# A new order table for all five engines of an attention and MLP kernel

## The chip, the core and the metric

The kernel runs on one core of a Trainium2 chip. The metric is the device time of one execution in microseconds (us). Before the change the median of three runs is 939.87 us (938.67 to 942.12).

TensorE (PE in the profile) multiplies matrices, VectorE (DVE), ScalarE (ACT) and GpSimd (POOL) work on tiles in SBUF and PSUM, and SyncE (SP) issues the DMAs. Each engine runs its own instructions strictly in order, and waits where an instruction's inputs or its buffer aren't ready.

## The reference

The reference has two parts. The first is attention with a window of 32 among 512 local tokens, joined by 32 global tokens that every local token sees and that see all 544. There are 8 batches, 8 heads and a head dimension of 64:

```python
s_ll = scale * np.matmul(q_l, k_l.transpose(0, 1, 3, 2))
s_ll = np.where(np.abs(pos[:, None] - pos[None, :]) <= 32, s_ll, -1000000000.0)
s_lg = scale * np.matmul(q_l, k_g.transpose(0, 1, 3, 2))
out_l = np.matmul(sm(np.concatenate([s_lg, s_ll], axis=-1)), np.concatenate([v_g, v_l], axis=2))
out_g = np.matmul(sm(scale * np.matmul(q_g, k_all.transpose(0, 1, 3, 2))), v_all)
```

Its output, 8 x 544 = 4352 tokens of 512 numbers, goes through an MLP with a cosine gate:

```python
h = x @ w_in          # 512 -> 2048
g = h * np.cos(h)
return g @ w_out      # 2048 -> 512
```

The weights come as 64-bit floats and are decoded on the chip into pairs of 16-bit floats (a high and a low part), and the inputs of most matmuls are such pairs too: a product takes three matmuls (high by high, high by low, low by high).

## The kernel before

**Attention.** A batch is handled as four pairs of heads (p = 0 to 3). Batches 0 and 1 run in the head of the program (functions f_*, fg_* and h_*; batch 0 wholly in 32-bit floats), while the weights are loaded and decoded. Batches 2 to 7 run in a steady pattern beside the MLP. For one pair: SyncE loads q and k (load_qk, L733); VectorE takes their largest magnitude (qk_a, qm at L818); TensorE spreads it over the partitions (spread_b at L796, into a PSUM tile pm_qk); ScalarE makes the high part qa (L857) and VectorE the low part kl (L858); four DMAs put the halves in place (qk_e, L869 to L874). Then, for each of four tiles of queries, TensorE makes the scores ps (sc_a, L1125 and L1126), VectorE adds the mask and takes the minimum mn of the negated scores (sc_b, L1142), which clears the PSUM tile; ScalarE takes the exponential and its sum (sc_c, by table_act at L715); POOL and ScalarE scale and split the result into plx (sc_d, L1171 to L1178); SyncE transposes it by DMA into ptb (sc_e, L1183); and TensorE multiplies by v into acc (av_a, L1215). ScalarE and VectorE write the MLP's input xh and xl (av_b, L1234 and L1235). The values v of a batch come in one load of 1280 KB (load_v, L781), and VectorE takes their maximum in four instructions (v_q, L897).

**MLP.** The tokens are cut into 17 chunks of 256, and the 2048 hidden units into 8 pieces (j). For chunk c and piece j, TensorE runs 24 matmuls into ph (m1_a, L1369); ScalarE and VectorE reduce the argument u of the cosine (m1_b, L1386 and L1387); ScalarE takes a sine (m1_c, L715); VectorE multiplies into gf (L1404), ScalarE rounds it to gh (L1408) and POOL makes the rest gl (L1409). Then 12 matmuls add to the output po (m2_a, L1423 to L1425), and after the last piece VectorE and ScalarE write o (m2_b, L1436 and L1438).

**Buffers.** PSUM has three tiles for ph, two for po and three that attention shares (ps, acc, pm_qk, gps and gacc). A tile is free when the engine that reads it last is done: ph when gf is made, ps when L1142 is done.

**Tables.** Exp and Sin lie in different tables of ScalarE. Wherever the two alternate in its order, the compiler puts in a load of the other table (ACT_TABLE_LOAD, at L715).

**What sets the order.** The body first issues the instructions step by step (a step is one call of one of the functions above). The table ORDER (L21), a line of numbers for each engine, then chains each engine's instructions:

```python
for name, line in ORDER.items():
    mine = [[i for i in step if i.engine == getattr(E_, name)] for step in steps]
    at_, prev, used = defaultdict(int), None, set()
    for word in line.split():
        word, _, times = word.partition("x")
        k, _, i = word.partition(".")
        at_[k] = int(i or at_[k])
        for _ in range(int(times or 1)):
            ins = mine[int(k)][at_[k]]
            at_[k] += 1
            if prev is not None:
                tc.add_manual_dep(ins, prev.name, order, reason="order")
            prev = ins
```

A word such as 23.4x2 means: of step 23, this engine's instruction 4 and the one behind it. So the table sets the place of every instruction, matmul, DMA issue and so on, on its own engine. What an instruction has to wait for on other engines follows from its data and its buffers, as before.

Of the kernel before, what the change touches and what calls it, by code (L numbers as in the profile page):

```python
# [22 lines left out]
        18x4 22x4 23.4 23.0 23.5 23.1x2 23.6 23.3 23.7 27x4 29.4x4 29.0x2 33 33.2 33.1 33.3 29x2 28x8  # L23
        34x8 35 35.4 35.1x3 35.5x2 40.4 49 35 40.0x2 40.5 40.2 40.6x2 40.3 57 39x8 69x4 41x8 74 74.2
        74.1 74.3 108 108.2 64x24 67x24 72x24 91x24 108.1 108.3 106x24 125x24 109 109.4 109.1 109.5
        109.2 109.6 109.3 109.7 135x7 110x2 110.4 110.2x2 110.5x3 135 143x6 112x8 113x4 124 127x4 141x8
        113x4 143x2 135x16 149x3 149.4 149.3 149.5x3 143x16 150 150.4 150.1 150.5 150.2 150.6 150.3
        150.7 151x8 155 155.4 155.1x3 152x8 156x20 157x8 164x8 189x5 189.6x5 189.5 189.11 164x16 170x5
        176x24 208 208.6x2 208.1x2 208.8x2 208.3x2 171x20 195x4 187x24 208 208.10x2 196 196.2 196.1
        196.3 206x19 227x24 229.6 206x5 229 229.0x3 229.8 229.3x2 229.9x3 229.5 250.6x2 250.0x2 250.8x3  # L30
        250.2x4 250.11 204 209x4 274x4 274.6x3 274.4 274.9x2 274.5 274.11 210x2 210.3 210.2 288.6x3
        288.0x6 288.9x3 300x4 300.6x4 300.4 300.10x2 300.5 230 231x8 233 233.2 233.1 233.3 248x24 272x24
        234 234.2 234.1 234.3 303.6 303.0x3 303.7x3 303.3x3 303.10x2 230x35 311x12 251 252x4 313x4 313.6
        313.4 313.7x5 313.5 253x4 251x35 318x5 318.6x2 318.5 318.8x4 325x3 325.6x6 325.3x3 275x12 276x8
        286x24 275x24 349x5 329x2 329.6 329.2x4 329.7x5 289x2 290 349x2 289x2 294x60 333.6x2 333.0x4
        333.8x2 333.4x2 333.10x2 289x32 307x60 319 322 339 339.6 339.1x2 339.7x2 339.3 339.9 349x17
        369x11 379x4 369x4 326x4 330x4 379x17 335x4 340x4 339x2 339.4x2 379x3 369x9 355x4 356x8 357
        351x2 351.6 351.2x2 351.7x3 351.4x2 351.10x2 371x4 372x8 392x24 407x24 421x24 382x4 394x12 433x2
        433.6x2 433.2 433.8x2 433.3x3 433.10x2 395x4 450.6x5 450.0x6 450.11 409x3 410 409 465.6x2
        465.0x4 465.8x4 465.4x2 394x24 431x24 424x3 435x4 424 448x24 463x24 436 451x3 452x4 479 481  # L40
        481.6 481.1x2 481.7x3 481.3x2 481.10x2 481.5 496 496.6x4 496.1x3 496.10 496.4x2 479x14 467x4
        468x8 479x9 482x4 494x19 496.11 494x5 483x8 489x60 451x33 497x2 498 512x24 529x24 497x2 514.6x2
        514.0 514.8x3 514.1x5 514.11 499x4 500 515x12 516x4 531 531.6 531.1x2 531.7 531.3 531.8x2 531.4
        531.10x2 531.5 517x4 544x21 546x4 546.6x4 546.4x2 546.10x2 533x4 562x24 550x4 583x24 544x3 564x3
        564.6 564.3x2 564.7 564.5 564.8x4 515x24 565x2 585.6x3 585.0 585.9x3 585.1x5 565x2 566x8 567 598
        598.6 598.1 598.7x4 598.2x4 598.11 612 612.6x3 612.1x3 612.9x3 612.4x2 596 586x36 587x4 588x8
        596x23 600x4 610x24 630 630.6 630.1 630.7 630.2x3 630.8x3 628x14 613x36 614x4 618x60 628x10
        643x24 631x4 651x24 630 630.5 645.6x4 645.0 645.10 645.1 645.11 645.2x4 632 653.6x3 653.0x3
        653.9x2 653.3x3 653.11 668x2 668.6 668.2 668.7 668.3x3 668.8x4 666x24 646x4 655x4 687x24 703x24
        673x36 674x4 689x3 689.6x2 689.3x3 689.8x3 690x4 689 691x8 705.6 705.0x4 705.7x2 705.4x2 705.9x3  # L50
        716x24 692 730x24 706x4 718.6x3 718.0 718.9x2 718.1 718.11 718.2x4 747x24 707x8 711x60 764x11
        720x4 733x36 734x4 750 732.6x5 732.0x3 732.11 732.3x3 764x13 749.6x3 749.0x2 749.9 749.2 749.10
        749.3 749.11 749.4x2 751 752 766 766.6x3 766.1x2 766.9 766.3x3 751x3 766.10x2 767x4 776x4 772x12
        787x17 774x3 772x12 807x24 787x7 774.6x6 774.3x3 793x36 794x4 789x3 789.6x2 789.3x3 789.8x2
        823x23 810x4 823 811x8 812 789x2 826x4 827x8 831x60 836x24 850x20 809x2 809.6x2 809.2 809.8x3
        809.3x3 809.11 840x4 866x24 850x4 825x5 825.6x4 825.5 825.10x2 838.6 838.0x2 838.7x5 838.2x4 852
        852.6x2 853x6 854x4 881x24 889x10 904x5 852.1x5 852.8x4 853x30 868x12 869x4 870 883x12 884x4
        889x14 891x12 893x4 904x19 906x12 911x36 912x4 925x24 927x12 928x4 929x8 930 941x24 943x12 944x4
# [1669 lines left out]
```

## Time and profile before

| | us |
|---|---|
| median of 3 runs | 939.87 (938.67 to 942.12) |
| the profiled execution | 944.08 |
| its span | 942.3 |
| PE busy | 886.3 (94%) |
| ACT busy | 677.5 (72%) |
| DVE busy | 585.8 (62%) |
| POOL busy | 495.3 (53%) |

The busy times are shares of the span and say nothing yet of which engine is waited for. The program has parts: up to about 50 us the weights are loaded and decoded beside batch 0's attention, up to about 216 us batches 0 and 1 and the first chunks run, then the steady pattern, and from about 792 us on little but the MLP's last chunks. The program has about 7900 matmuls, and each engine's instruction has a line in kernel.py by which the views name it.

### The profile page before, as it was taken

Reading aid. Unit: us, or ns where it says so; the run is one execution under the profiler, and the core shown is the slowest. Engines: PE = TensorE matmul, PEld = TensorE weight load, DVE = VectorE, ACT = ScalarE, POOL = GpSimd, SP = SyncE. Lnnn points to the kernel's source line nnn. Section 1 sums busy time; section 2 is a strip of 40 time slices with the busy share of each in tenths; the row PEclk is TensorE's granted clock in tenths of the full one; section 3 lists DMA queues with packets and bytes.
Section 4 is the critical chain, followed back from the end, with each engine's and each line's share of the span. In section 5 each row is a group of like instructions: output and inputs, shape, how many; then the busy total and the mean of one; then the engine's idle time right before and its main releaser. Section 6 shows DMA issues by size and latency. Waiting matters only on the chain.

```text
span 942.3 us, 20875 instructions
## 1 busy us (share of the span) xinstructions
PE 886.3 (94%) x7892; PEld 611.9 (65%) x7892; DVE 585.8 (62%) x1536; ACT 677.5 (72%) x1331; POOL 495.3 (53%) x731
## 2 busy tenths in 40 slices
PE   5689988789999999999999999989999999999998
PEld 4468745466766776756767667657767766666673
DVE  5998885778765776776676667665765444223230
ACT  4789988779998878967876777767787774444441
POOL 3477889815766455466562546555656552121220
PEclk9779999999999999999999999999999999999999
DMA  9774615875667466476456655645554421000000
GB/s 339 274 235 169 213 23 125 156 192 105 149 146 137 128 120 132 108 158 121 104 127 141 135 99 124 163 85 134 92 109 85 93 42 42 1 23 13 12 24 23
DMA packets 162422, 110.79 MB, mean 118 GB/s; under 512 B 140176, under 2 KB 142608, under 8 KB 160400
## 3 DMA queue, kind: packets, MB, share of 16 engines
q1 hardware_dynamic: 162176, 109.31, 47.8%
q8 instruction: 62, 1.02, 0.4%
q14 instruction: 40, 0.33, 0.1%
q10 hardware_dynamic: 144, 0.13, 0.1%
HBM read 51.61 MB, written 8.91 MB: 64 GB/s over the span
## 4 chain that ended last, share of the span: by engine, by line
PE 48%; ACT 16%; DVE 12%; DMA 10%; POOL 5%; issue 4%; SPq 1%; DVEq 0%; POOLq 0%; ACTq 0%
PE ph L1369 21%; PE po L1425 7%; PE po L1423 7%; PE po L1424 7%; ACT t L715 3%; DMA qkr<-qk 3%; ACT u L715 2%; DMA vr<-v 2%; ACT L715 2%; DVE u L1387 2%; PE acc L1215 2%; DMA ptb<-plx 1%; DVE gf L1404 1%; ACT u L1386 1%; ACT gh L1408 1%
## 5 line engine op out<-in xcount | busy, mean ns | idle before, releaser
L1369 PE MATMUL ph<-xh,wi_h 128*128 128x256 f16 x1024 | 281.5, 275 | 8.5 <-DVE gf L1404 7.5
L1369 PE MATMUL ph<-xl,wi_h 128*128 128x256 f16 x1024 | 281.7, 275 | 0.0
L1369 PE MATMUL ph<-xh,wi_l 128*128 128x256 f16 x1024 | 281.4, 275 | 0.4 <-POOL wi_l L457 0.4
L1409 POOL TENSOR_TENSOR gl<-gf,gh 128x512 f16<-128x512 f32 x136 | 159.4, 1177 | 226.2 <-ACT gh L1408 222.0
L1369 PEld LDWEIGHTS <-wi_h 128*128 128x128 f16 x2176 | 212.0, 99 | 49.5 <-issue 12.1
L1424 PE MATMUL po<-wo_l,gh 128*128 128x512 f16 x544 | 203.9, 379 | 1.5 <-POOL wo_l L457 1.5
L1423 PE MATMUL po<-wo_h,gh 128*128 128x512 f16 x544 | 201.5, 379 | 3.2 <-DVE o L1436 2.3
L1425 PE MATMUL po<-wo_h,gl 128*128 128x512 f16 x544 | 201.5, 379 | 1.6 <-POOL gl L1409 1.6
L1387 DVE SCALAR_TENSOR_TENSOR u<-ph,ca,u 128x512 f32<-128x512 f32 x136 | 101.2, 745 | 114.9 <-ACT u L1386 114.6
L715 ACT ACTIVATE t<-t,mn 128x224 f32<-128x224 f32 (+1 forms) x256 | 118.2, 463 | 51.6 <-DVE mn L1142 35.9
L1171 POOL TENSOR_SCALAR t<-t,sm 128x224 f32<-128x224 f32 (+1 forms) x192 | 85.3, 462 | 127.4 <-DVE sm L1162 104.0
L715 ACT ACTIVATE u<-u,halfpi 128x512 f32<-128x512 f32 x136 | 97.1, 720 | 61.8 <-DVE u L1387 61.2
L1404 DVE SCALAR_TENSOR_TENSOR gf<-u,ph 128x512 f32<-128x512 f32 x136 | 92.8, 684 | 76.5 <-ACT u L715 65.6
L1386 ACT ACTIVATE u<-ph,quarter,ca 128x512 int32<-128x512 f32 x136 | 103.9, 767 | 46.4 <-PE ph L1369 46.1
L1178 POOL TENSOR_TENSOR plx<-t,plx 128x192 f16<-128x192 f32 (+1 forms) x192 | 120.9, 654 | 24.5 <-ACT plx L1176 24.0
L1369 PEld LDWEIGHTS <-wi_l 128*128 128x128 f16 x1088 | 107.4, 99 | 14.5 <-POOL wi_l L457 0.6
L1408 ACT CAST gh<-gf 128x512 f16<-128x512 f32 x136 | 82.6, 614 | 46.2 <-DVE gf L1404 46.1
L1425 PEld LDWEIGHTS <-gl 128*128 128x128 f16 x544 | 53.2, 98 | 67.1 <-POOL gl L1409 2.5
L1424 PEld LDWEIGHTS <-gh 128*128 128x128 f16 x544 | 53.2, 98 | 55.2 <-issue 4.2
L715 ACT ACT_TABLE_LOAD x67 | 86.0, 1283 | 2.6 <-DVE gmn L768 1.4
L1423 PEld LDWEIGHTS <-gh 128*128 128x128 f16 x544 | 52.9, 98 | 52.3 <-issue 2.3
L1142 DVE CUSTOM_DVE_ANT_0 t<-ps,msk,al 128x192 f32<-128x192 f32 (+1 forms) x192 | 76.5, 427 | 9.5 <-PE ps L1126 9.3
(239 smaller groups left out, 1223.5 us busy)
## 6 DMA issues: line engine op xcount, KB each, us to landing
qkr<-qk SPq DMA_DIRECT2D x24, 608.0 KB, 4.5
vr<-v SPq DMA_DIRECT2D x8, 1280.0 KB, 6.6
out<-o SPq DMA_DIRECT2D x33, 256.0 KB, 2.0
kh<-qa SPq DMA_DIRECT2D x48, 152.0 KB, 2.7
wo_h<-wo SPq DMA_DIRECT2D x8, 512.0 KB, 4.5
wo_l<-wo SPq DMA_DIRECT2D x8, 512.0 KB, 4.3
qa<-kl SPq DMA_DIRECT2D x24, 152.0 KB, 2.5
kl<-kl SPq DMA_DIRECT2D x24, 152.0 KB, 3.1
```

The costliest lines, as they stand in the source:

```text
L715: ins = nc.scalar.activation(*a, **k).ins
L1171: nc.gpsimd.tensor_scalar(t[:, h], t[:, h], r[:, h : h + 1], 1.0, op0=ALU.mult, op1=ALU.mult)
L1178: nc.gpsimd.tensor_tensor(lo[:, h], t[:, h], hi[:, h], op=ALU.subtract)
L1369: nc.tensor.matmul(ph[:, a], w[:, kc, f], x[:, kc, q], start=first and ip == 0, stop=last and ip == 2, skip_group_check=True,)
L1386: nc.scalar.activation(u.bitcast(I32), ph, AF.Identity, bias=quarter, scale=a)
L1387: nc.vector.scalar_tensor_tensor(u, ph, a, u.bitcast(I32), op0=ALU.mult, op1=ALU.subtract)
L1404: nc.vector.scalar_tensor_tensor(gf, w, 0.5, st.pop(("ph", c, j)).rearrange("p a b -> p (a b)"), op0=ALU.mult, op1=ALU.mult,)
L1408: nc.scalar.copy(gh, gf)
L1409: ins = nc.gpsimd.tensor_tensor(gl, gf, gh, op=ALU.subtract).ins
L1423: nc.tensor.matmul(po[k], gh[:, q], wo_h[:, f], start=(f == 0), stop=False)
L1424: nc.tensor.matmul(po[k], gh[:, q], wo_l[:, f], start=False, stop=False)
L1425: nc.tensor.matmul(po[k], gl[:, q], wo_h[:, f], start=False, stop=(f == NJ - 1))
```

## The change

Only the numbers in ORDER change, for all five engines. The arithmetic, the tiles, the buffers, the DMAs and the steps are the same. The table is 34 lines longer, so that each line number behind it is larger by 34 in the changed kernel (L1142 is L1176 there). From the middle of the program on, the old table for TensorE is a regular pattern (24 matmuls of one piece, 12 of another, and so on), and the new one is mixed more finely. Two pieces of the table, whose other lines are of the same kind:

```diff
--- before.py
+++ after.py
@@ -20,217 +20,251 @@
 ORDER = {
     "PE": """
-        18x4 22x4 23.4 23.0 23.5 23.1x2 23.6 23.3 23.7 27x4 29.4x4 29.0x2 33 33.2 33.1 33.3 29x2 28x8
-        34x8 35 35.4 35.1x3 35.5x2 40.4 49 35 40.0x2 40.5 40.2 40.6x2 40.3 57 39x8 69x4 41x8 74 74.2
...
+        18x4 22x4 23.4 23.0 23.5 23.1x2 23.6 23.3 23.7 27x4 29x8 33.1 33.3 33.0 33.2 28x8 35 35.4 34x8
+        35.1x3 35.5 40 40.4 40.1 40.5 40.2 40.6x2 49 35 40.3 57 35 39x8 69x4 41x8 74 74.2 74.1 74.3 108
...
     "SP": """
-        0.1 0.0 6 2x2 4x2 1 5 3 7 6 8 9 10 11 12 13.1 13.0 78 14x2 17 79 15.1 15.0 81 77 16.1 172 16.0
-        17 80 172 82 83 84 98 99 100 101 102 103 104 105 122 123 119 175 120 175 121 116 173 174 173 117
...
+        0.1 0.0 1 2x2 3 5 4 8 4 7 6x2 9 10 11 12 13.1 13.0 15 14 77 14 16x2 15 78 81 80 79 172.1 117
+        17.1 84 17.0 82 116 83 98 119 118 100 172.0 99 101 102 104 103 105 120 121 173 175x2 173 122 123
...
```

What that does is shown at three places. The first is SyncE's queue at the start of the program: qkr, qf and kf are the queries and keys of batch 0, msk the mask, and wi and wo the weights, loaded into tiles that are used for other things later. Before:

```order
L777 DMA qkr_0_0_118<-qkf 128x352 x2
L777 DMA qf_0_3_132<-qkf 128x352
L777 DMA qf_0_1_122<-qkf 128x352
L777 DMA kf_0_1_123<-qkf 128x352
L777 DMA qf_0_2_127<-qkf 128x352
L777 DMA kf_0_2_128<-qkf 128x352
L1514 DMA msk_73<-mask 128x896
L583 DMA plx_76<-wi 128x1024
L583 DMA wo_h_92<-wi 128x1024 x2
L777 DMA kf_0_3_133<-qkf 128x352
L583 DMA vhl_77<-wi 128x1024
```

And now:

```order
L811 DMA qkr_0_0_118<-qkf 128x352 x2
L1548 DMA msk_73<-mask 128x896
L811 DMA qf_0_1_122<-qkf 128x352
L811 DMA kf_0_1_123<-qkf 128x352
L617 DMA wo_h_92<-wi 128x1024
L617 DMA plx_76<-wi 128x1024
L811 DMA qf_0_2_127<-qkf 128x352
L617 DMA vhl_77<-wi 128x1024
L811 DMA kf_0_2_128<-qkf 128x352
L617 DMA wo_h_92<-wi 128x1024
```

The mask is issued third instead of eighth, and the first loads of w_in stand among those of q and k.

The second is VectorE round the maximum over batch 7's v (vm4_7 from vr_7), beside the clearing of the scores of batch 6's second pair (ps_6_1_2 and ps_6_1_3) and chunk 10 of the MLP (u_10, gf_10). Before:

```order
L1142 ISA t_6_1_2_8687,mn_6_1_2_8688<-ps_6_1_2_8678,msk_73,al_6_1_8109 128x224
L1142 ISA mn_6_1_2_8688 128x1
L787 TENSOR_SCALAR qm_7_0_9128<-qm_7_0_9128 128x1
L427 TENSOR_SCALAR qm_7_0_9128<-qm_7_0_9128 128x1
L897 TENSOR_REDUCE vm4_7_9543<-vr_7_9079 128x1 x4
L1387 SCALAR_TENSOR_TENSOR u_10_1_8726<-ph_10_1_8701,ca_10_8627,u_10_1_8726 128x512
L901 TENSOR_REDUCE vm_7_9542<-vm4_7_9543 128x1
L787 TENSOR_SCALAR vm_7_9542<-vm_7_9542 128x1
L1142 ISA t_6_1_2_8687,mn_6_1_3_8783<-ps_6_1_3_8778,msk_73,al_6_1_8109 128x192
L1142 ISA mn_6_1_3_8783 128x1
L1142 ISA t_6_1_2_8687,mn_6_1_3_8783<-ps_6_1_3_8778,msk_73,al_6_1_8109 128x192
```

And now the place where the maximum stands:

```order
L1421 SCALAR_TENSOR_TENSOR u_10_4_8993<-ph_10_4_8968,ca_10_8627,u_10_4_8993 128x512
L1176 ISA t_6_2_2_9021,mn_6_2_2_9022<-ps_6_2_2_9010,msk_73,al_6_2_8458 128x224
L1176 ISA mn_6_2_2_9022 128x1
L1470 TENSOR_SCALAR o_9_1_9077<-po_9_1_8424,co_8_8319 128x512
L931 TENSOR_REDUCE vm4_7_9543<-vr_7_9079 128x1 x2
L1421 SCALAR_TENSOR_TENSOR u_10_5_9060<-ph_10_5_9035,ca_10_8627,u_10_5_9060 128x512
L1176 ISA t_6_2_2_9021,mn_6_2_2_9022<-ps_6_2_2_9010,msk_73,al_6_2_8458 128x224
L1176 ISA mn_6_2_2_9022 128x1
L1438 SCALAR_TENSOR_TENSOR gf_10_4_9031<-u_10_4_8993,ph_10_4_8968 128x512
L1389 TENSOR_SCALAR co_12_11271<-osc_99,pvs_101 128x1
L1176 ISA t_6_2_2_9021,mn_6_2_3_9123<-ps_6_2_3_9118,msk_73,al_6_2_8458 128x192
```

The four instructions of the maximum stand behind the scores of the third pair's tile 1 (ps_6_2_1) now, where before they stood ahead of the second pair's tile 3 (ps_6_1_3); they are in two pairs, of which the second comes later still. On SyncE the load of vr_7 stood ahead of kl_6_2's last move and stands behind it now.

The third is ScalarE in chunk 10, with the exponentials of batch 6's second pair (t_6_1) and the sines of chunk 10 (u_10). Before:

```order
L1386 ACTIVATE u_10_0_8661<-ph_10_0_8636,quarter_83,ca_10_8627 128x512
L715 ACTIVATE u_10_0_8661<-u_10_0_8661,halfpi_85 128x512
L715 ACT_TABLE_LOAD
L715 ACTIVATE t_6_1_0_8460,sm_6_1_8794<-t_6_1_0_8460,mn_6_1_0_8461 128x192 x2
L715 ACTIVATE t_6_1_1_8558,sm_6_1_8794<-t_6_1_1_8558,mn_6_1_1_8559 128x224 x2
L1408 CAST gh_10_0_8695<-gf_10_0_8697 128x512
L715 ACTIVATE t_6_1_2_8687,sm_6_1_8794<-t_6_1_2_8687,mn_6_1_2_8688 128x224 x2
L1386 ACTIVATE u_10_1_8726<-ph_10_1_8701,quarter_83,ca_10_8627 128x512
L1234 ACTIVATE xh_6_8786<-acc_6_0_8741,xs_95 128x512
L715 ACTIVATE t_6_1_2_8687,sm_6_1_8794<-t_6_1_2_8687,mn_6_1_3_8783 128x192 x2
L715 ACTIVATE gt_6_0_8464,gsm_6_0_8803<-gt_6_0_8464,gmn_6_0_8465 128x544
```

And now:

```order
L749 ACT_TABLE_LOAD
L749 ACTIVATE u_10_0_8661<-u_10_0_8661,halfpi_85 128x512
L749 ACT_TABLE_LOAD
L749 ACTIVATE t_6_1_1_8558,sm_6_1_8794<-t_6_1_1_8558,mn_6_1_1_8559 128x224 x2
L749 ACTIVATE t_6_1_2_8687,sm_6_1_8794<-t_6_1_2_8687,mn_6_1_2_8688 128x224
L1268 ACTIVATE xh_6_8786<-acc_6_0_8741,xs_95 128x512
L1442 CAST gh_9_7_8630<-gf_9_7_8632 128x512
L749 ACTIVATE t_6_1_2_8687,sm_6_1_8794<-t_6_1_2_8687,mn_6_1_2_8688 128x224
L1420 ACTIVATE u_10_2_8838<-ph_10_2_8813,quarter_83,ca_10_8627 128x512
L749 ACT_TABLE_LOAD
L749 ACTIVATE u_10_1_8726<-u_10_1_8726,halfpi_85 128x512
L749 ACT_TABLE_LOAD
```

Before, the four pairs of exponentials and one gt stood between two sines (the second load comes right behind the last row); now a sine stands between smaller groups of them, and four table loads stand in the piece shown instead of one. In the whole program there are 94 loads instead of 68.

## Rows read from the trace of the kernel before

**Rows 1.** The page, the span in 40 slices: TensorE's granted clock, in tenths.
```profile
PEclk9779999999999999999999999999999999999999
```

**Rows 2.** Busy time by stretch: us, engines (instructions), PEclk, DMA share, GB/s.
```profile
0.00:216.00 216.00, 176.68 (x1528) 124.03 (x1529) 168.25 (x461) 171.66 (x353) 145.00 (x228) 0.94 0.62 189
72.00:144.00 72.00, 67.42 (x599) 47.71 (x598) 59.88 (x148) 67.51 (x140) 60.03 (x87) 0.99 0.41 136
216.00:408.00 192.00, 186.35 (x1820) 131.79 (x1819) 137.76 (x379) 167.84 (x332) 110.62 (x166) 1.00 0.61 131
408.00:624.00 216.00, 209.56 (x1960) 144.40 (x1958) 142.40 (x384) 156.64 (x317) 116.57 (x175) 0.99 0.56 123
...
624.00:936.00 312.00, 312.00 (x2583) 211.08 (x2582) 136.90 (x317) 180.89 (x330) 123.15 (x163) 1.00 0.27 58
```

**Rows 3.** Waits of TensorE over the span: total us, times, longest us.
```profile
PE ftr L1008 <- POOL dg L993: 11.3, 6, 4.4
PE ph L1369 <- DVE gf L1404: 7.5, 8, 1.6
PE acc L1215 <- DMA ptb<-plx: 5.2, 5, 1.5
...
PE pm_qk L796 <- DVE mn L1142: 3.1, 2, 2.5
PE ps L1126 <- DMA kl<-kl: 3.0, 4, 1.3
```

**Rows 4.** Timeline of SyncE's queue, 594 to 620: start us, us, engine, instruction.
```profile
606.38 0.54 SPq L781 DMA_DIRECT2D vr<-v  x1
610.46 0.46 SPq L874 DMA_DIRECT2D kl<-kl  x1
```

**Rows 5.** Timeline of VectorE, 596 to 620, idle time and its releaser in brackets.
```profile
614.16 3.00 DVE L897 TENSOR_REDUCE vm<-vr 128x1 f32<-128x640 f32 x4 [2.63 <-DMA vr<-v]
...
617.99 0.41 DVE L1142 CUSTOM_DVE_ANT_0 t<-ps,msk,al 128x192 f32<-128x192 f32 x1
```

**Rows 6.** Timeline of TensorE, 612 to 622.
```profile
612.26 0.27 PE L1369 MATMUL ph<-xh,wi_h 128*128 128x256 f16 x1
612.37 0.27 PE L1369 MATMUL ph<-xl,wi_h 128*128 128x256 f16 x1
...
618.80 0.22 PE L796 MATMUL pm_qk<-ident,qm 128*128 128x128 bf16 x1 [2.47 <-DVE mn L1142]
...
619.58 0.42 PE L1369 MATMUL ph<-xl,wi_h 128*128 128x256 f16 x1
619.79 0.42 PE L1369 MATMUL ph<-xh,wi_l 128*128 128x256 f16 x1
```

**Rows 7.** Busy time by stretch, two stretches in the middle.
```profile
602.80:706.00 103.20, 100.73 (x943) 69.97 (x941) 68.91 (x186) 76.65 (x156) 55.28 (x82) 0.98 0.55 121
616.00:624.00 8.00, 5.53 (x34) 3.82 (x32) 6.32 (x20) 5.53 (x12) 4.04 (x9) 0.79 0.01 2
```

**Rows 8.** Timeline of VectorE in the head.
```profile
8.70 0.45 DVE L966 CUSTOM_DVE_ANT_0 t<-fps,msk,alf 128x224 f32<-128x224 f32 x1 [6.07 <-DMA msk<-mask]
...
12.79 1.22 DVE L524 TENSOR_REDUCE wm<-plx 128x1 f32<-128x1024 f32 x1 [1.03 <-DMA plx<-wi]
```

**Rows 9.** Timeline of SyncE's queue in the head.
```profile
4.03 0.43 SPq L1514 DMA_DIRECT2D msk<-mask  x1
```

**Rows 10.** The page, costliest groups: busy us, mean ns, idle before.
```profile
L715 ACT ACT_TABLE_LOAD x67 | 86.0, 1283 | 2.6 <-DVE gmn L768 1.4
```

**Rows 11.** Timeline of ScalarE, 600 to 622.
```profile
605.99 1.28 ACT L715 ACT_TABLE_LOAD   x1
607.28 0.45 ACT L715 ACTIVATE t<-t,mn 128x192 f32<-128x192 f32 x1
...
610.57 0.62 ACT L1408 CAST gh<-gf 128x512 f16<-128x512 f32 x1 [1.37 <-DVE gf L1404]
```

**Rows 12.** Waits of ScalarE over the span.
```profile
ACT u L715 <- DVE u L1387: 61.2, 56, 3.3
```

More of the change, by code (lines that the diff above doesn't have):

```diff
@@ new lines @@
+        318.6x2 318.5 318.8x4 275x5 276x8 325x3 325.6x6 325.3x3 286x24 275x31 349x4 329x2 329.6x6
+        329.2x4 289 290 294x60 289x8 369x8 333.6 349x4 333 333.0x4 333.8x2 333.4x2 333.10x2 289x14
+        307x60 289x13 319 322 339 339.6 339.1x2 339.7x2 339.3 339.9 339.4x2 339.10x2 349x16 351.6 369x16
+        379x10 326x4 330x4 335x4 379x12 340x4 351.0x2 351.7 351.2x2 351.8x2 351.4 355 351.10 379x2 356x8
+        351.5 351.11 357 355x3 371x4 372x8 392x24 407x24 382x4 433x2 433.6x2 433.2 433.8x4 433.3x3
@@ new lines @@
+        1027x12 1047x5 1047.6x5 1047.5 1047.11 1031x36 1032x4 1061x3 1074x2 1061 1048x4 1061x19 1049x8
+        1074 1061 1050 1074x21 1064x4 1065x8 1069x60 1063x2 1063.6x2 1063.2x3 1063.8x4 1063.5 1088x24
+        1078x4 1076.6x2 1076.0 1076.8x3 1076.1x4 1076.11 1076.5 1090.6x3 1090.0x6 1090.9x3 1104x24
+        1091x36 1092x4 1106 1106.6x6 1106.1x5 1119x24 1121x2 1121.6x6 1121.2x4 1107x4 1108 1129x2
+        1129.6x2 1129.2x4 1129.8x4 1127x24 1144x3 1144.6 1142x24 1163x14 1179x9 1122x4 1163x10 1144.3
@@ new lines @@
+        1382.10x2 1380x24 1401x24 1387x36 1388x4 1403x4 1403.6x6 1403.4x2 1417x24 1404x2 1405x8 1404x2
+        1430x24 1406 1419.6 1419.0 1419.7x3 1419.1x2 1419.10x2 1419.3x3 1420x4 1432x2 1421x8 1425x60
+        1434 1444x24 1432.6x5 1432.2x2 1432.11 1432.4x2 1461x15 1434x3 1447x36 1448x4 1461x9 1446x4
+        1446.6x6 1446.4x2 1478x24 1463x3 1464 1465x4 1466 1486x24 1463.6 1463.3x2 1463.7x4 1463.5
+        1463.11 1481x4 1490x4 1480.6x4 1480.0x5 1480.10 1480.5 1480.11 1501x24 1488.6x3 1488.0 1488.9x3
@@ new lines @@
+        1488.1x5 1521x24 1507x36 1508x4 1537x13 1503 1503.6 1503.1 1503.7x5 1503.2x4 1550x10 1524x4
+        1525x8 1537x11 1550x5 1526 1550x3 1540x4 1523x2 1523.6x3 1523.2x3 1523.9x3 1523.5 1550x6 1539
+        1539.6x5 1539.1 1539.11 1539.2x4 1564x24 1541x8 1545x60 1580x13 1552.6 1552.0x5 1552.7x4 1554x4
+        1580x11 1552 1552.5 1567x36 1566x3 1566.6x4 1566.3x3 1566.10x2 1568x4 1595x24 1603x24 1583
+        1582.6x3 1582.0x4 1582.9x3 1582.4x2 1597x2 1597.6x3 1597.2x3 1597.9x2 1597.5 1597.11 1617x24
@@ L119 @@
[L119 to L121 removed]
[4 rows of a table removed]
+        20x4 25x4 44x2 23 31x4 29x2 47 48 37 48 37 48 47 48 23 37x2 53 40.1 53 35x2 40.0 56x2 59 93x2 66
+        93x2 60 94 61 66 62 71 94x3 76 65 85 71 68 73 76 97 88 86 87 97 89 92 107 129 97 126 130 109 97
@@ L234 @@
+        1668 1632 1720 1709 1721 1705 1707 1706 1633 1708 1768 1769 1814 1860 1861 1882 1815 1892
     """,
```

390 lines of the change are left out of this document (197 added, 193 removed), and 19 rows, old and new, of the table ORDER.

## The prediction

> **What bounds the kernel now.** I read the clock row of the page first, then the busy times by stretch, then TensorE's waits, and last the timelines round the two waits that the change touches. The clock row is at 9 in nearly every slice [rows 1], so TensorE's speed is given and only its idle time and short dips can be won. The stretches [rows 2] show where it idles: 216.00 - 176.68 = 39.3 us in the head (0 to 216 us), 5.65 + 6.44 = 12.1 us in 216 to 624, and nothing in 624 to 936 (312.00 busy of 312.00). These 51.4 us are what an order can win, besides dips of the clock and a tail of a few us. The matmuls are the same instructions in both orders, so their own time stays.
>
> The waits of TensorE [rows 3] have no single owner: 11.3 us on POOL's diagonals in the head, 7.5 us on a free ph buffer, 5.2 on transposes, 3.1 on a free buffer for pm_qk, 3.0 on kl. In 408 to 624 the worst is one event. SyncE issues the 1280 KB load of v at 606.38, ahead of kl at 610.46 [rows 4]; VectorE reaches the maximum over v, idles 2.63 us for that load, runs 3.00 us from 614.16, and only at 617.99 clears the scores whose buffer pm_qk needs [rows 5]. TensorE stands 2.47 us before 618.80, and then its matmuls come 0.21 us apart instead of 0.11 [rows 6]. The granted clock of 616 to 624 is 0.79 [rows 7]: 8 x 0.21 = 1.7 us more. So this one event costs 2.5 + 1.7 = 4.2 us.
>
> The trace is of an execution of 944.08 us (span 942.3, 1.8 outside), 4.2 above the median of 939.87. The change is summed against 944.08 and then taken off the median; nothing in the changed order touches what lies outside the span.
>
> **The change part by part.** No arithmetic and no DMA is added or removed; each engine's instructions come in another order. The only instructions that come and go are ScalarE's table loads, put in wherever Exp and Sin alternate: 68 in the program before, 94 now.
>
> *Head.* The mask is SyncE's third DMA now, not its eighth. VectorE waits 6.07 us for it, until 8.70 [rows 8]. It is issued at 4.03 and an issue takes 0.43 [rows 9], 0.47 with the gap behind it, so without five of them it can come 5 x 0.47 = 2.4 us earlier. But at 12.79 VectorE waits again, 1.03 us, for the first piece of w_in [rows 8], and that piece isn't here any sooner; so 1.4 of the 2.4 count. The w_in loads keep their order among the small loads, and the last two of them stay behind all others, so the weights should not be here earlier. On ScalarE three table loads stand between the first u of chunk 0 and that of chunk 1 where five stood: 2 x 1.28 = 2.6 us [rows 10], and ScalarE is 94% busy in 72 to 144 [rows 2], so there it counts. Sum 1.4 + 2.6 = 4.0 gained. The bounds are wide, because the whole head is moved: a fifth of the 39.3 us idle (8 us) won at best, and at worst one more wait like the longest on the diagonals, 4.4 us [rows 3]. I take -4, worked out from the only two rows that I can tie to a moved instruction.
>
> *216 to 624.* The load of v is issued behind kl now, the maximum is cut into two pairs, and both pairs stand behind the clearing of the scores that pm_qk needs, some 13 us of VectorE work later. The event of 4.2 us should go, and with it the other wait of the pm_qk row (3.1 - 2.5 = 0.6 us [rows 3]), so 4.8. What is late next there is the next ph buffer, freed by gf, whose 8 waits are 1.6 us at most [rows 3]; VectorE has 2.63 us of idle time there [rows 5] to be early with it, so I take nothing off. The waits on kl (3.0 us) and on transposes (5.2 us) are a matter of how much TensorE work lies between an issue and its use. The new order puts more between for some (kl of batch 3's third pair, the transposes of batch 4's first) and less for others (kl of batch 4's first pair, the transposes of batch 3's third and fourth). I take half of 8.2, 4.1. Sum about 9 gained. Ends: 12.1 + 1.7 = 13.8, all that is lost in this stretch, and 0, if each removed wait comes back behind another buffer. 9 is nearer to the first since the largest event has a named cause that the order takes away.
>
> *624 to 936.* Here nothing can be won, only lost. Between the first u of chunk 10 and the first u of chunk 12 ScalarE had 120 instructions, 8 of them table loads; it has 138 now, 20 of them loads. The cost: 12 x 1.28 = 15.4 us [rows 10], and six more (three gh, two Sin, one cast) of about a gh's 0.62 us [rows 11], 3.7. Before, this stretch ran from 602.80 to 706.00 with ScalarE busy 76.65 us [rows 7]; now it would have 76.65 + 19.1 = 95.8 us. TensorE's part of it is 103.2 less the event of 4.2 us, less about 2 us of matmuls that the new order puts elsewhere: 97 us. ScalarE would have to be busy 99% of the time. How full can it run? The fullest stretch in the trace is 72 to 144, at 67.51 / 72 = 93.8%; 216 to 408, where TensorE keeps 97%, has 167.84 / 192 = 87% [rows 2]. At 93.8% the stretch takes 95.8 / 0.938 = 102 us, 5 over TensorE's. Some of that is taken up by buffers: ph has three, so ScalarE can fall behind by two groups of 24 matmuls (2 x 24 x 0.11 = 5.3 us) before TensorE waits, and behind chunk 12 it has time again. The ends are 0 (all taken up) and, at 80% full, 95.8 / 0.80 - 97 = 23 us. I take 4, from the row of 93.8%, since that is the stretch where ScalarE was itself pressed. Chunks 6 to 9 get 27 loads where 17 stood, 12.8 us, beside 216 - 156.64 = 59 us of idle ScalarE in 408 to 624 [rows 2]: nothing, and 12.8 if that cover were gone. Chunks 12 and 13 get 14 where 6 stood, 10 us, also beside an idle ScalarE (180.89 busy of 312 in 624 to 936 [rows 2]).
>
> The trace shows a switch of table as 1.28 us and the next ACTIVATE starting 1.29 us after the load started [rows 11]. The Trainium skill, "ScalarE: Activation LUTs", section "What ACT_TABLE_LOAD costs", puts a drain of about 1.38 us on top, 2.66 us for each switch. By that rule the 26 new loads would take 69 us of ScalarE, by the row 33; the row is of this kernel and decides, and no gap of that size stands in it.
>
> *Tail.* The last chunk's output matmuls lie farther from the matmuls that feed them than before, and TensorE waited for nothing there up to 936 [rows 2]. Nothing.
>
> **The sum.** -4 - 9 + 4 = -9: 944.08 - 9 = 935.1 for the profiled execution, and 939.87 - 9 = 930.9 as a median. I say 931.
>
> **Rivals.**
>
> *No change.* Each removed wait comes back at the next buffer, or ScalarE in chunks 10 and 11 runs no fuller than 87%: 95.8 / 0.87 - 97 = 13 us lost, which is just what head and middle gain: -13 + 13 = 0, 940. For it: TensorE's waits have many owners [rows 3], none of them long. Against it: the largest event has one cause, and that moves.
>
> *Slower: ScalarE becomes the engine that all wait for in chunks 10 and 11.* Exp and Sin alternate there one by one, and each change of table also fixes an order: a Sin behind an Exp that waits for VectorE waits too, and TensorE's ph buffers are freed by that Sin's gf. Over the whole span ScalarE idled 61.2 us before Sins that waited for VectorE's u [rows 12]. At 81% full the stretch takes 95.8 / 0.81 = 118 us, 21 over; -13 + 21 = +8: 948. It decides from the point at which ScalarE is less than about 83% full in this stretch (18 us over TensorE's 97, which is the gain of 13 and 4.7 more). Against it: a stretch of 94% exists. For it: there TensorE was busy only 67.42 of 72 us [rows 2].
>
> *A switch of table holds ScalarE for longer than its row.* Were it twice 1.28 us, the 20 loads of that stretch would make it 95.8 + 25.6 = 121 us even with ScalarE never idle, 24 over TensorE's: -13 + 24 = +11, 951. [rows 11] speak against it, with no time between a load and the next Exp; I give it 0.02, inside the slower case. The Trainium skill's page named above states such a rule, and the trace disagrees with it here.
>
> *All of it works.* The head gains 8, the middle 13, ScalarE's loads cost nothing: -21, 919. For it: the 51.4 us of idle time. Against it: I can name causes for only a quarter of them.
>
> *The order doesn't do what it is made for:* DMAs land later than it assumes, so that the slack behind them is eaten. vr took 7.8 us from issue to use [rows 4, 5]; the order gives it some 13. This ends with no change, and is counted there.
>
> **How the numbers follow.** A measurement of this kernel can tell 0.5%, 4.7 us, from no change. Forecast, 922 to 935: 0.46. All of it works, 912 to 922: 0.14. No change, 935 to 945: 0.23. Slower, above 945: 0.17. So faster 0.60, same 0.23, slower 0.17. The range from 914 to 947 leaves out about 0.05 below and 0.13 above; the likeliest case's own range is 922 to 935.
>
> **What would show it.** Right: the maximum over v no longer stands before TensorE's wait on pm_qk, and no dip of the clock near the middle; TensorE's idle time in what was 216 to 624 falls from 12 to some 4 us; ScalarE busy about 33 us more in all (677 to about 711), and above 90% full in chunks 10 and 11 with TensorE idle there for under 6 us. Wrong: TensorE waits for gf or for a free ph buffer again and again in chunks 10 and 11; or the first matmul of chunk 0 starts later than before; or the waits on transposes and kl are as many as they were.

## The result, and the profile after

The changed kernel takes 926.1 us (median of four runs, 925.04 to 927.98), the kernel before 940.37 beside it: a ratio of 0.985 with a 95% interval of 0.9825 to 0.9876, so 14.3 us less. The forecast was 931, in a range of 914 to 947. The profiled execution of after took 926.73 us with a span of 924.9, against 944.08 and 942.3 of before. That is 17.4 us of span; about 3 us of them are there only because the profiled execution of before lies 3.7 us above its median, and that of after 0.6.

Busy time by stretch in the changed kernel, with the columns of [rows 2] (engines with their instructions, then granted clock, DMA share and GB/s):

```profile
0.00:216.00 216.00, 185.33 (x1625) 130.91 (x1627) 179.88 (x494) 182.60 (x381) 151.56 (x240) 0.96 0.67 201
...
216.00:408.00 192.00, 190.85 (x1878) 136.05 (x1876) 136.29 (x379) 167.84 (x328) 112.93 (x175) 1.00 0.63 134
408.00:624.00 216.00, 209.14 (x1966) 144.72 (x1965) 134.20 (x373) 177.56 (x339) 108.27 (x165) 0.99 0.59 123
616.00:624.00 8.00, 5.67 (x58) 3.56 (x57) 5.49 (x16) 5.44 (x14) 0.06 (x1) 0.81 0.68 168
624.00:919.00 295.00, 294.24 (x2427) 198.39 (x2426) 124.06 (x291) 177.62 (x311) 113.69 (x153) 1.00 0.23 49
```

TensorE idles 30.7 us up to 216 (39.3 before), 1.2 + 6.9 = 8.0 in 216 to 624 (12.1 before) and 0.8 behind that. A program that does the same work sooner shows other work in the same stretch, so I also laid the two profiled executions side by side by TensorE's work done (each matmul at the spacing its rows show): at the work that before has done by 217 us, after is 13.8 us ahead; at 636 us of before it is 22.4 ahead; 20 us later 18.3, and 17.4 at the end. Three things, then: a lead won in the head, a second one won in the middle, and about 4 us lost again. These are leads of one execution over one other; what of them other executions show stands under e4 and e8.

What TensorE waits for (total us, times, longest), as in [rows 3]:

```profile
PE acc L1249 <- DMA ptb<-plx: 8.5, 11, 2.3
PE acc L1067 <- ACT ptb L1046: 7.2, 3, 5.7
PE ph L1403 <- DVE gf L1438: 4.6, 5, 1.6
...
PE ftr L1042 <- POOL dg L1027: 3.2, 3, 2.1
```

The rows for kl are gone (3.0 before), the one for pm_qk is down from 3.1 to 0.4 and 0.2, on other instructions, and POOL's diagonals from 11.3 to 3.2. The transposes are the largest wait now, 8.5 instead of 5.2, and at 29 us there is one of 5.7 on ScalarE's ptb, whose row was 1.4 in all before. What VectorE waits for at loads has nearly vanished. Before:

```profile
DVE qm L818 <- DMA qkr<-qk: 39.9, 14, 4.3
DVE vm L897 <- DMA vr<-v: 11.1, 4, 3.4
DVE t L966 <- DMA msk<-mask: 6.1, 1, 6.1
```

After (no row for v or the mask is left; the 17.1 us on the output end at 617, 767 and 901 us, and TensorE waits for VectorE at none of these three places):

```profile
DVE o L1470 <- DMA out<-o: 17.1, 3, 12.6
...
DVE qm L852 <- DMA qkr<-qk: 1.7, 1, 1.7
```

So the slack behind the DMAs is real: 57 us of VectorE's waits for loads became 1.7 there. What that is worth is another matter (e9).

The 4 us that are lost again lie at 617 to 624 us. The chain of waits of the changed kernel there (start, us, what):

```profile
599.64 0.34 SPq L815
600.05 9.48 DMA qkr<-qk
609.56 1.43 DVE qm L852
...
613.59 1.05 POOL plx L1212 x2
...
616.23 3.37 DMA ptb<-plx
619.64 1.36 PE acc L1249 x36
```

L815 at 599.64 is the load of batch 7's v. The load qkr stands right behind it and takes 9.5 us to land, where the median of these loads is 4.7; VectorE idles for it, clears the scores late, and TensorE waits 2.3 us for the last transpose. The granted clock of 616 to 624 is 0.81 behind that wait, as it was 0.79 before [rows 7]: part of the stretch is at the lower of TensorE's two levels, 1.2 GHz. The load that held up VectorE at the maximum over v before [rows 5] holds it up at the maximum over qkr now.

ScalarE's table loads, and the stretch from the first u of chunk 10 to the first u of chunk 12 in the changed kernel:

```profile
L749 ACT ACT_TABLE_LOAD x93 | 119.3, 1283 | 1.5
```

```profile
575.84:684.27 108.43, 105.27 (x965) 71.92 (x963) 70.74 (x191) 95.56 (x173) 57.49 (x85) 0.98 0.53 112
```

ScalarE is busy 95.56 us in it, as the prediction worked out (95.8), but the stretch is 108.4 us long, and TensorE alone is busy for 105.3 of them. ScalarE is 88% full, not 99%.

### The profile page after: what moved, and what is told of

Read it like the earlier page. It is cut to its first block, busy times and chain, and to the rows that moved or that the text cites. A ratio compares the mean times of both kernels' runs of the same rounds, so it can differ in the third digit from the quotient of the medians.

```text
span 924.9 us, 20747 instructions
## 1 busy us (share of the span) xinstructions
PE 880.9 (95%) x7892; PEld 610.5 (66%) x7892; DVE 574.9 (62%) x1536; ACT 706.1 (76%) x1357; POOL 486.4 (53%) x731
## 4 chain that ended last, share of the span: by engine, by line
PE 56%; ACT 8%; DMA 5%; DVE 5%; POOL 3%; issue 2%; SPq 1%; ACTq 0%; DVEq 0%; POOLq 0%
PE ph L1403 25%; PE po L1457 8%; PE po L1458 8%; PE po L1459 8%; DMA ptb<-plx 4%; PE acc L1249 3%; ACT t L749 2%; ACT L749 1%; PE ps L1159 1%; PE ps L1160 1%; DMA qkr<-qk 1%; ACT u L749 1%; POOL gl L1443 1%; ACT u L1420 1%; ACT qa L891 1%
## 5 line engine op out<-in xcount | busy, mean ns | idle before, releaser
L1443 POOL TENSOR_TENSOR gl<-gf,gh 128x512 f16<-128x512 f32 x136 | 162.1, 1203 | 152.9 <-ACT gh L1442 137.0
L1458 PE MATMUL po<-wo_l,gh 128*128 128x512 f16 x544 | 200.4, 380 | 0.3 <-POOL wo_l L491 0.3
L1459 PE MATMUL po<-wo_h,gl 128*128 128x512 f16 x544 | 197.2, 380 | 0.0
L1457 PE MATMUL po<-wo_h,gh 128*128 128x512 f16 x544 | 196.4, 381 | 0.0
L1205 POOL TENSOR_SCALAR t<-t,sm 128x192 f32<-128x192 f32 (+1 forms) x192 | 86.1, 465 | 155.4 <-DVE sm L1196 97.9
L1212 POOL TENSOR_TENSOR plx<-t,plx 128x192 f16<-128x192 f32 (+1 forms) x192 | 109.5, 595 | 43.8 <-ACT plx L1210 41.0
L1176 DVE CUSTOM_DVE_ANT_0 t<-ps,msk,al 128x192 f32<-128x192 f32 (+1 forms) x192 | 77.2, 429 | 48.6 <-PE ps L1160 48.2
```

The source lines that it names most:

```text
L1205: nc.gpsimd.tensor_scalar(t[:, h], t[:, h], r[:, h : h + 1], 1.0, op0=ALU.mult, op1=ALU.mult)
L1212: nc.gpsimd.tensor_tensor(lo[:, h], t[:, h], hi[:, h], op=ALU.subtract)
L1443: ins = nc.gpsimd.tensor_tensor(gl, gf, gh, op=ALU.subtract).ins
L1457: nc.tensor.matmul(po[k], gh[:, q], wo_h[:, f], start=(f == 0), stop=False)
L1458: nc.tensor.matmul(po[k], gh[:, q], wo_l[:, f], start=False, stop=False)
L1459: nc.tensor.matmul(po[k], gl[:, q], wo_h[:, f], start=False, stop=(f == NJ - 1))
```

## The experiments

Each kernel ran beside the kernel before; "before" is that chip's median. The first four share a median of 940.92 us for before.

**e1 and e2: the two halves.** From the traces I know when each engine ran each instruction. A set of all that ran before some moment can be put first, and the rest behind it in the other order. At 189 us of after and 200 us of before the two sets are nearly the same.

```diff
 for each engine:
-old order
+e1: [ran before 189 us in after, new order] + [the rest, old order]
+e2: [ran before 200 us in before, old order] + [the rest, new order]
```

> The table of before, but with every engine's instructions that ran in the first 189 us of the changed kernel put first, in the new order; the rest follows in the old order. At that seam the two orders have done almost the same work (12 instructions differ, 2.7 us of them), the new one 11 us sooner. Theory A, the gain is local: what the new order wins up to 189 us is kept, as nothing behind it depends on the new order. 940.4 - 11 = 929 (927 to 932). Theory B, the lead is given back: the steady part of the old order waits for DMAs and buffers that don't come sooner. 936 to 940.

> The other half: every engine's first 200 us of the old order, and then the new order for the rest. Theory A, the gain is local: only what the new order wins behind 200 us is left, 17.4 - 11 = 6.4, so 940.4 - 6.4 = 934 (932 to 936). Theory B, the steady part is where the whole gain is made and the head's lead is only passed on: 926 to 930.

e1 took 933.76 (0.9915, 0.9889 to 0.9941), 7.2 us less than before; e2 934.18 (0.9931, 0.9913 to 0.995), 6.7 less. The sum, 13.9, is within the noise the gain of the whole change (14.3). So the gain is local: head and rest each keep their own, and neither passes on nor eats the other's. By size e1 is short of theory A (933.8 for 929): its seven-odd us are the 7.5 us of lead that its own profiled execution has at 209 us. The seam lies ahead of the 216 us at which the prediction ends the head: e2's profiled execution goes from 1.2 to 4.0 us of lead between 189 and 217 us of before, so that nearly 3 us of its gain belong to the head too.

**e3: the new order for the first 61 us alone.**

```diff
+e3: [ran before 61 us in after, new order] + [the rest, old order]
```

> The new order for what ran in the first 61 us of the changed kernel (weights loaded and decoded, batch 0's attention), and the old order behind it. At this seam the new order is 4 us ahead. Theory A, the weights' decoding and the waits between 150 and 217 us gain separately: 4 us are kept, 940.4 - 4 = 936.4 (935 to 938), and TensorE's waits on po, ptb, kl and ph between 150 and 217 us stand as in the kernel before. Theory B, the early lead is what empties those later waits: 929 to 932. Theory C, ScalarE and POOL, not TensorE, set the time behind 70 us, and the lead is lost there: 939 to 941.

940.72 (0.9993, 0.9978 to 1.0009): nothing is kept (by the interval, at most 2 us), theory C. By TensorE's work done e3 is 3.2 us ahead at 62 us of before and 1.1 at 76. What the new order wins while the weights are decoded is lost again some 10 us later.

**e12: the new order from 110 to 189 us alone.**

```diff
+e12: [ran before 110 us in before, old order] + [what ran up to 189 us in after, new order]
+     + [the rest, old order]
```

> The old order to 110 us, the new one for all engines for what runs from there to 189 us of the changed kernel, and the old one again. e3 showed that the lead of the first 61 us is not kept. Theory A, the gain of e1 is made where VectorE waits for tiles that POOL frees (9.3 us in 110 to 190 before, 3.0 after) and TensorE for what comes of it: all of e1's 7 us, 933 to 935. Theory B, it is made between 61 and 108, by two table loads fewer and POOL's earlier start on batch 1: 938 to 941.

936.47 beside 942.09 (0.9948, 0.9929 to 0.9967): 5.6 us, most of e1's 7.2. It lies between the ranges of the two theories; theory A holds as to the place, for the larger part. Busy time of 110 to 190, before and e12:

```profile
110.00:190.00 80.00, 68.83 (x582) 41.05 (x580) 59.01 (x156) 68.48 (x147) 71.45 (x113) 1.00 0.51 111
```

```profile
110.00:190.00 80.00, 74.84 (x670) 44.66 (x670) 57.61 (x163) 69.64 (x149) 70.53 (x114) 0.98 0.58 123
```

TensorE is busy 6.0 us more in the same 80 us (with the clock at 0.98 for 1.00, so that a part of it is slower matmuls), while POOL, the fullest engine there before, is about as busy as it was. By TensorE's work done e12 is 0.1 us ahead at 110 us of before, 3.8 at 189 and 5.7 at 209. What TensorE no longer waits for in this stretch are the inputs and the buffer of po, 4.7 us; before:

```profile
PE po L1423 <- DVE o L1436: 1.6, 1, 1.6
PE po L1425 <- POOL gl L1409: 1.6, 2, 1.1
PE po L1424 <- POOL wo_l L457: 1.5, 1, 1.5
```

None of the three is left in e12, and the wait for transposes falls from 2.0 to 0.7. The wait for gf stays:

```profile
PE ph L1369 <- DVE gf L1404: 2.3, 2, 1.6
```

```profile
PE ph L1369 <- DVE gf L1404: 2.0, 1, 2.0
```

VectorE's longest wait in this stretch before, and the same wait in e12:

```profile
DVE t L966 <- POOL plx L760: 9.3, 6, 5.4
```

```profile
DVE t L966 <- POOL plx L760: 3.0, 2, 2.6
```

VectorE stood in its own order behind a score tile that POOL had yet to free. Which of TensorE's waits hung on that is not shown, nor that it makes the 5.6 us: the experiment changes all engines in this stretch, and the waits that went end at VectorE's o and at POOL's gl and wo_l.

**e10, e11 and e13: one engine at a time.** The new order of the first 189 us for TensorE alone (e10), for the four others (e11), and for SyncE alone (e13).

```diff
 first 189 us:
+e10: PE new;  Activation, DVE, Pool, SP old
+e11: Activation, DVE, Pool, SP new;  PE old
+e13: SP new;  PE, Activation, DVE, Pool old
```

> As e1, the new order for what ran in the first 189 us of the changed kernel and the old one behind, but for TensorE alone; ScalarE, VectorE, POOL and SyncE keep the old order throughout. e1 gained 7.2 us. Theory A, TensorE's own order makes it: matmuls of chunks 1 and 2 stand where it waited for transposes, gl and o. 933 to 935. Theory B, what the other engines do first makes it, as their results come sooner: TensorE's new order alone waits as long in other places, 939 to 943.

> The complement of e10: in the first 189 us the new order for ScalarE, VectorE, POOL and SyncE, and the old order for TensorE. Theory A (TensorE's order makes the gain of e1): 939 to 943. Theory B (the other engines' order makes it): 933 to 935. If the two need each other, both kernels stay near 940.

> The new order of the first 189 us on SyncE's queue alone (the mask third instead of eighth, the loads of w_in and w_out and the transposes of batches 0 and 1 moved), all other engines in the old order. The prediction gave the mask 1.4 us by itself: 939.5 by that. Rival, as e3 has it: the head's early leads are lost again by 75 us: 940.5 to 941.5. A difference of 1.4 us is about what five rounds can tell.

All three miss every theory. Beside 942.09 for before, e10 took 975.94 (1.0371, 1.0348 to 1.0394), e11 951.8 (1.0115, 1.0093 to 1.0138) and e13 960.39 (1.0213, 1.0183 to 1.0243): 34, 10 and 18 us slower, where all engines together are 7 us faster. In e10 TensorE now stands at a matmul whose input POOL makes later (11.3 us before [rows 3]):

```profile
PE ftr L1008 <- POOL dg L993: 22.2, 8, 8.3
PE ph L1369 <- DVE gf L1404: 9.8, 8, 2.9
```

In e11 TensorE's old order asks for ph buffers that VectorE's new order has not yet freed (7.5 us before [rows 3]):

```profile
PE ph L1369 <- DVE gf L1404: 16.4, 7, 6.5
```

In e13, whose profiled execution of 966.64 us is 6 us above its median, VectorE asks for loads in an order in which they no longer come:

```profile
13.80 1.22 DVE L524 TENSOR_REDUCE wm<-plx 128x1 f32<-128x1024 f32 x1 [5.17 <-DMA plx<-wi]
```

```profile
194.79 0.82 DVE L897 TENSOR_REDUCE vm<-vr 128x1 f32<-128x640 f32 x1 [6.10 <-DMA vr<-v]
```

The mask is early in e13: VectorE starts on its first scores at 5.57 us instead of 8.70, and then, in its old order, waits 5.2 us instead of 1.0 [rows 8] for a piece of w_in that the new queue issues behind another. So the mask's 1.4 us by itself are not measured; what e13 shows is that these moves on SyncE lose without the consumers' order that goes with them. The waits are not the whole loss: for the same matmuls TensorE is busy 12.5 us longer in e10 (898.8 for 886.3) and 9.8 in e13, where the granted clock of 0 to 216 is 0.84 and 0.90 instead of 0.94.

**e4: the load of v and its maximum alone.** SyncE's and VectorE's parts of the table for batch 7 (batch 6 likewise, with its own numbers; 1386 is the load, 1339 kl's last move, 1451 the maximum, 1331 the scores, 1343 and 1356 u and gf):

```diff
 SP
-1377 1322 1386 1339 1370
+1377 1322 1339 1386 1370
 DVE
-1391x2 1451x4 1327 1451x2 1331x2 1451 1332 1349x2 1353x3 1341 1353 1343 1348
+1391x2 1327 1331x2 1332 1349x2 1353x3 1341 1353 1343 1451x2 1348
```

> The table of before with one edit, for batches 6 and 7: SyncE issues the load of v behind kl's last move, and VectorE takes the maximum over v some 10 us later, behind the clearing of the scores that pm_qk's buffer waits for. The prediction's step: the wait of 2.47 us before pm_qk6_3 goes, with the slower matmuls behind it, and batch 6's 0.6 us: -4.8, so 935.6 (934.5 to 937.5). Rival: the wait comes back at the next buffer or the later maximum delays batch 7's v: 939 to 942.

936.62 (0.9954, 0.9937 to 0.997), 4.3 us less for 4.8 expected. The wait on pm_qk is gone from the list. By TensorE's work done the profiled execution gains 4.3 us over that of before at the place of the event, from 5.2 to 9.5, and gives 1.6 back at once, at po of chunk 10, where TensorE waits for ScalarE's o to clear the buffer:

```profile
633.34 0.38 PE L1423 MATMUL po<-wo_h,gh 128*128 128x512 f16 x1 [1.43 <-ACT o L1438]
```

But 4.2 us is what the event cost in that one execution of before. In e3, where the order of this stretch is the old one too, TensorE waits at the same matmul and the clock does not fall behind it:

```profile
618.27 0.22 PE L796 MATMUL pm_qk<-ident,qm 128*128 128x128 bf16 x1 [2.29 <-DVE mn L1142]
```

```profile
616.00:624.00 8.00, 5.73 (x42) 4.04 (x42) 6.32 (x22) 6.06 (x13) 4.56 (x10) 1.00 0.01 2
```

In e1, e10, e12 and e13, old order there as well, the wait is 1.2, 1.9, 1.6 and 1.0 us, and the clock of the 8 us round it is 1.00 each time; in e11 there is no wait. All of them then wait 0.7 us at po of chunk 10, where before does not. So e3 loses 3.0 us here (2.29 and 0.72), and e4 still loses 1.4: without the dip, which only the execution of before has, the edit saves some 1.6 us at batch 7. The rest comes from batch 6, where the prediction counted 0.6 us: between 500 and 550 us of before e4's lead grows from 2.8 to 5.4 and e3's by nothing; with the wait on pm_qk (0.7 us) two of 0.7 us at po are gone there, for ScalarE's o and for VectorE's o.

**e9: e4, and all other waits of VectorE for qkr in batches 5 to 7.** For one of the eleven maxima:

```diff
 DVE
-1431 1511 1443 1439x2 1511x2 1445 1449x2 1450 1470x2 1474x3
+1431 1443 1439x2 1445 1449x2 1450 1470x2 1511x3 1474x3
```

> The table of before with the edit of e4 and one more: VectorE takes each maximum over q and k (qm) of batches 5, 6 and 7 about 7 us later (the first pair's by 2 us), still over 20 us ahead of its use, so that it no longer waits 2 to 4 us for each load; in all VectorE idles 43 us for these loads and for v in 420 to 700. Theory A, slack behind each DMA is what the middle's gain is made of: about 9 us, 931 to 933. Theory B, VectorE's idle time costs nothing but at the one place that e4 mends: 936 to 937.

935.56 beside 941.72 (0.9946, 0.9925 to 0.9967): 6.2 us less than before, where e4 had 4.3; it lies between the ranges of the two theories, and the intervals of e9 and e4 overlap nearly whole. VectorE's waits fell as meant:

```profile
DVE qm L818 <- DMA qkr<-qk: 5.9, 3, 3.8
DVE vm L897 <- DMA vr<-v: 4.8, 2, 3.3
```

They were 39.9 and 11.1, and 38.1 and 4.6 in e4. So taking away 32 us of VectorE's idle time behind loads was worth about 2 us, if anything; in the trace the wait of 1.43 us at po of chunk 10 is gone. That is nearer to theory B: that idle time costs something where TensorE waits for what stands behind it, and hardly anywhere else.

**e6 and e7: the table loads.** An exponential in place of the sine, in chunks 10 and 11 (e6) or in all (e7).

```diff
-            table_act("Sin", w, w, AF.Sin, scale=TWOPI, bias=halfpi)
+e6:         table_act("Sin", w, w, AF.Exp if c in (10, 11) else AF.Sin, scale=TWOPI, bias=halfpi)
+e7:         table_act("Sin", w, w, AF.Exp, scale=TWOPI, bias=halfpi)
```

> The changed kernel with an exponential in place of the sine in chunks 10 and 11 (so those two chunks' values are other ones): same instructions of the same size in the same order, but 20 table loads fewer, 74 instead of 94, all of them in the stretch that the prediction charged with +4 us. Theory A, the prediction's term: the loads press ScalarE there and cost TensorE about 4 us. 926.1 - 4 = 922. Theory B, the loads hide; the 4 us that the changed kernel loses at 617 to 624 us (2.6 us before acc_6_1 and slower matmuls behind it) hang on the load of v ahead of qkr on SyncE. 925 to 927, and the wait for ptb before acc_6_1 is still there.

> The changed kernel with an exponential in place of every sine (all chunks' values are other ones): no table loads but the first, same instructions otherwise. 93 x 1.28 = 119 us of ScalarE go. Theory A, ScalarE is what the others wait for in the head and in chunks 6 to 13: 4 us there and 3 to 6 in the head, where it is 92% busy from 72 to 144 us: 916 to 919. Theory B, ScalarE's loads lie beside other work nearly everywhere: 923 to 926.

e6 took 928.87 beside 941.72 (0.9872, 0.9846 to 0.9899), e7 924.9 (0.9831, 0.9804 to 0.9857); after is at 0.985. Twenty loads fewer gain nothing (928.9 lies above the ranges of both theories, and TensorE still waits 2.68 us before acc_6_1), and 93 fewer, 119 us of ScalarE, about 1 us, which is within the noise. Theory B. In e7 ScalarE has 63% of the span instead of 76%, and TensorE still waits for the same thing:

```profile
PE acc L1249 <- DMA ptb<-plx: 8.7, 11, 2.1
```

**e8: qkr ahead of v.**

```diff
 SP
-1322 1339 1386 1377 1368.1 1368.0
+1322 1339 1377 1386 1368.1 1368.0
```

> The changed kernel with one edit on SyncE: the load of batch 7's v (1280 KB) is issued behind qkr_7_0 (608 KB) instead of right ahead of it. In the changed kernel qkr_7_0 lands 9.5 us after its issue, VectorE waits 1.7 us for it at 609.6, the scores behind it are cleared late, and acc_6_1 waits 2.4 us for the last transpose. Theory A, that chain: 2 to 4 us less, 922 to 924. Theory B, ScalarE's late u (with three table loads ahead of it), for which VectorE waits 2.8 us just before, sets the same chain: 925.5 to 927.

924.74 beside 941.72 (0.9829, 0.9805 to 0.9852), between the ranges of the two theories. The wait and the slower clock at 616 to 624 are gone, and the transposes' row falls from 8.5 to 5.9:

```profile
616.00:624.00 8.00, 8.00 (x88) 5.92 (x87) 5.81 (x16) 7.09 (x16) 1.49 (x2) 1.00 0.76 151
```

```profile
PE acc L1249 <- DMA ptb<-plx: 5.9, 12, 0.8
```

By the trace theory A's chain is right: e8 is 20.0 us ahead of before at 636 us and still 19.9 at 656, where after goes from 22.4 to 18.3. The medians show 1.4 us (924.7 for 926.1, each beside its own runs of before), and the intervals of the ratios overlap, so that e8 beats the changed kernel is likely and not shown. Nor do other executions of the new order lose 4 us here: e2 waits 1.60 us at this matmul and e7 2.06, both with the clock at 1.00 behind it, and lose 1.6 and 2.1. The 1.7 us of slow matmuls are there in after and in e6.

## Why the prediction was right, point by point

- *What can be won is TensorE's idle time and dips of its clock* [rows 2, 7]. Right: its idle time, but for the tail, fell by 12.0 us (51.4 to 39.4). The matmuls' own time, which was to stay, fell by 5.4 as well (886.3 to 880.9 busy for the same matmuls), with the granted clock of 0 to 216 at 0.96 for 0.94.
- *Head, -4.* Too small: 7.2 in e1, nearly 3 more behind e1's seam, and 13.8 in the two profiled executions. The step that failed was to count only what could be tied to a moved instruction. The mask came early (VectorE takes its first scores at 5.65 instead of 8.70 [rows 8]) and two table loads went, but e3 keeps nothing of the first and e7 shows the second to cost about nothing. The first matmul of chunk 0, which needs the weights, starts at 47.3 us for 50.9, though the prediction held that the weights would not be here earlier; in e3 it starts at 48.6, and nothing of that is kept either. What gained, for the larger part, is 110 to 189, where the prediction had no term. One row from 0 to 216 [rows 2] hid it: TensorE's idle time in 144 to 216 is 11.9 us before and 2.3 after.
- *216 to 624, -9.* Right in sum (8.6 by TensorE's work done, up to 614 us of after), its parts less so. The prediction read 4.2 us for the event off one execution; 1.7 of them, the dip of the clock, are in none of the six other executions of the old order there, and 1.4 come back at po. The 4.8 for batches 6 and 7 came out, 4.3 in e4, because batch 6's part is worth 2.6 and not 0.6. The 4.1 for kl and transposes was right by chance: kl's 3.0 went, the transposes' wait grew by 3.3, and ph's and po's waits fell (ph from 7.5 to 4.6).
- *624 to 936, +4 for table loads.* A loss of this size is in the profiled execution (4.1), and its cause is another. ScalarE's work was right to 0.3 us; the 97 us for TensorE's part of the stretch were not. The prediction took 2 us of matmuls off; between the two u of ScalarE lie 104 us of TensorE's work in the new order, with 18 matmuls of po and 4 of ps more than before, so ScalarE had 12% to spare. e6 and e7 rule the loads out as its cause, since the wait at 617 to 624 stays without them, and e8 names the load of v. The rival on table loads that hold ScalarE longer than their row falls with e7 too. The Trainium skill, "ScalarE: Activation LUTs", section "Table sets: the hidden batching unit", advises to do all of one table's functions before the other's; no run here shows a gain from that, and the kernel with 26 loads more is the faster one.
- *What would show it.* In part. ScalarE's table loads took 33.3 us more, as said, and it is busy 28.6 us more in all (706.1 for 677.5). In chunks 10 and 11 TensorE idles 3.2 us, under 6 as said, but ScalarE is 88% full there, not above 90%, and TensorE's idle time in 216 to 624 fell from 12.1 to 8.0, not to 4. Of the signs of being wrong one came up by half: the waits for kl are gone, but TensorE waits for transposes 11 times where it did 5 times. The dip of the clock in the middle, which was to go, came back at the same place for another reason.

Between the two profiled executions the terms are -13.8, -8.6 and +4.1, with another 0.9 lost behind: -17.4, for -4, -9 and +4. So nearly the whole miss is the head, which was taken too small; that +4 charged to loads which cost nothing meets a loss of 4.1 to a transfer and a slow clock is luck, and some 3 of the 17.4 us are not in the medians. 931 for 926.1 is therefore closer than its terms.

What stays open: which of the moved instructions in 110 to 189 make its 6 us. TensorE's waits at po go there, and VectorE's wait for POOL is shorter, but neither was taken away by itself, and engine by engine the first 189 us can't be split, since each part alone is slower.

## What to carry to other kernels

An order of instructions is one thing over all engines: a part of it is tested along time, by putting first what ran up to some moment, and not engine by engine, where parts of a gain of 7 us came out as losses of 10 to 34. An event that one trace shows is priced once a second execution shows it too: of 4.2 us read here, 1.7 were of that one execution. An in-order engine's wait for a DMA is worth moving where the bounding engine waits for what is queued behind it; 32 us of other such waits were worth about 2. A small load that is needed soon goes ahead of a large one on the same queue (in e8 the wait for it went; the gain of about 1 us is not clear of the noise). Before a full engine is charged with a stretch, the length of that stretch is taken between the same two instructions on both sides.

## What the runs showed of the hardware

- A load of 608 KB issued 0.4 us behind one of 1280 KB on the same queue took 9.5 us to land; the median of these loads in the same execution is 4.7.
- TensorE's clock does not fall behind every wait of about 2 us. Behind the wait of 2.33 us in after, the granted clock of 616 to 624 is 0.81 and the matmuls of po, 0.216 us apart at 2.4 GHz, come 0.43 apart, at 1.2 GHz:

```profile
619.64 1.36 PE L1249 MATMUL acc<-ptb,vhl 128*64 128x128 f16 x36 [2.33 <-DMA ptb<-plx]
...
621.53 0.63 PE L1457 MATMUL po<-wo_h,gh 128*128 128x512 f16 x1
621.96 0.63 PE L1458 MATMUL po<-wo_l,gh 128*128 128x512 f16 x1
```

  Behind the same instruction in e7, after a wait of 2.06 us, the stretch 616 to 624 is at 1.00:

```profile
620.94 1.36 PE L1249 MATMUL acc<-ptb,vhl 128*64 128x128 f16 x36 [2.06 <-DMA ptb<-plx]
```

```profile
616.00:624.00 8.00, 5.94 (x74) 4.57 (x72) 4.95 (x13) 3.00 (x10) 1.14 (x2) 1.00 0.89 211
```

  At pm_qk likewise: 0.79 behind 2.47 us in the execution of before [rows 6, 7], 1.00 behind 2.29 us in e3. What parts these cases is not shown.
